# A planner's priorities for one block's chain, a seventh half piece beside it, and three unused matmuls fewer

## The chip, the cores and the metric

The kernel runs on one core of a Trainium2 chip. The metric is the device time of one execution in microseconds (us). Before the change it is 488.02 us, the median of three runs (486.81 to 488.70).

The engines that matter: TensorE (PE in the profile; PEld is its weight load), VectorE (DVE), ScalarE (ACT), GpSimd (POOL) and SyncE (SP), whose queue issues nearly all transfers.

## The reference

The operation has two halves. Half A is a convolution branch: `h = layernorm(x) * (1 + ca) + sa`, a short causal filter of four taps on `k`, `kv = k_shift * v`, a causal convolution of `kv` with a filter of length 2048 along the sequence (written with an FFT), and `x = x + ga * h * (conv + kv * ssm_D)`. Half B is a gated feed-forward network:

```
h   = layernorm(x) * (1 + cb) + sb
out = (silu(h @ w1) * (h @ w3)) @ w2
x   = x + gb * out
```

The six vectors sa, ca, ga, sb, cb, gb are the six parts of `silu(c) @ w_mod`. The sequence has 2048 rows of width 576, the hidden width is 4608, all in bf16.

## The kernel before

**Tiling.** The sequence is cut into eight blocks of 256 rows. The long convolution is done block by block in a small transform space: each block of `kv` gets a spectrum X (six rows of 576 per partition), each block of the filter a spectrum V, and block s of the result is the inverse transform of the sum over X[i] * V[s - i]. VectorE makes those products and sums (`pair`, tiles of 128x3456 elements: `p`, `z`), TensorE the forward and inverse transforms as matmuls with bases `Fk`, `Fb`, `Fi`.

The feed-forward half goes by row blocks of 512 rows, so two sequence blocks share one round r of four. In `stream`, w1 and w3 come in nine pieces of 512 columns (`wst` buffers 0, 1, 2, and in round 0 two more in the room of the spectra). For each piece TensorE makes gate and up in PSUM, ScalarE writes silu(gate) (`h`) and copies up (`u`), and VectorE multiplies them. In `down`, w2 comes in nine pieces of 288 KB per half of the output width, VectorE multiplies the result by gb (`og`, `gbrow`) and adds it to x. The matmuls of `stream` use half of the array's rows at a time: 64 rows, two of them side by side.

**The first round.** Round 0 needs block 0 and block 1. Only block 0 is ready early (`first_block`, an order written out by hand). So the stream of round 0 begins with half pieces: six of the nine w1/w3 pieces are run on the first 256 rows alone (matmuls of 256 columns), while block 1's convolution (`conv_second`) is in the works. When block 1's normalised rows (`h2row`) have been transposed by TensorE and written, scaled, to `h2T`, the same six pieces are run on rows 256 to 511, and the other three on all 512 rows. `FIRST` is the order in which round 0's `down` takes the hidden columns, `jobs` the order of the pieces.

**Block 1's chain.** `kv_rows` (VectorE) makes kv; `x_spectrum` (TensorE, copies by ScalarE) its spectrum; `x_sums`, `pair`, `real_parts` (VectorE) the product in transform space; `inverse` (TensorE); `residual_row` (VectorE, tiles `hg` and `x`); `quick_stats` (VectorE, GpSimd) and `normed` (VectorE) the rows `h2row`; `turn_split` and `turned_split` the transposes and the writing of `h2T`. Beside it, `filter_ahead(2)` makes the filter spectrum for block 2, and `mod_piece(5)` makes `gbrow` with ten matmuls of w_mod's last part, which `load_gb` brings into buffer 2.

**What sets the order.** After `first_block` all instructions are recorded and ordered by a planner (`_Recorder`). `relate` finds what each unit of work must come after. `weigh` gives the matmuls of the two streams (the lanes) their due times one after the other, and each other unit the latest start that its followers allow (`latest`). `search` runs `plan` a hundred times with noise on these due times and keeps the order with the best modelled time. `plan` fills each engine by readiness and then by `latest`. What comes out is a fixed order per engine; each engine works strictly in it and waits on semaphores. SyncE waits, for each transfer, on whatever last used the target and on the transfer eight places before it.

`mod_columns`, in `first_block`, turns two rows of the modulation into columns with small matmuls (`one,Wo` in the profile); `warm` puts matmuls before each of them whose result nobody reads (`shk`).

Of the kernel before, what the change touches and what calls it, by code (L numbers as in the profile page):

```python
# [22 lines left out]
H = 288  # L23
NF = F // P
RB = 512
NRB = S // RB
FC = 4
NW13 = 3
W2C = 4
N1 = 24  # L30
SPLIT = 2
AHEAD = 2
EPS = 1e-5
FIRST = (2, 3, 4, 5, 6, 0, 7, 1, 8)


def _ap(t, offset, dims):
# [173 lines left out]

class _Unit:
    def __init__(self, engine, n, fixed):
        self.engine, self.n, self.fixed = engine, n, fixed
        self.ops, self.pair = [], None
        self.lane, self.swap = False, None
        self.before, self.behind = set(), set()
        self.takes, self.uses = [], []
        self.start = self.end = None
        self.latest = float("inf")  # L220
        self.parts = []
# [16 lines left out]
class _Recorder:  # L238
# [23 lines left out]
    def __init__(self, tc):  # L262
        self.tc, self.nc = tc, tc.nc
        self.tiles, self.units = [], []
        self.fixed, self.open = True, None
        self.homes = {}
        for e in self.NAMES:
            setattr(self, e, _Engine(self, e))

    def add(self, op):  # L270
        u = self.open
        if u is None:
            u = _Unit(op.engine, len(self.units), self.fixed)
            self.units.append(u)
        assert u.engine == op.engine
        u.ops.append(op)

    @contextmanager
    def together(self, lane=False, swap=None):
        assert self.open is None  # L280
        self.open = u = _Unit("tensor", len(self.units), self.fixed)
        u.lane, u.swap = lane, swap
        self.units.append(u)
        try:
            yield u
        finally:
            self.open = None
# [63 lines left out]
    def relate(self):  # L351

        log = {}

        def meets(a, b):
            return a[1] < b[2] and b[1] < a[2] and any(x[0] < y[1] and y[0] < x[1] for x in a[3] for y in b[3])

        def inside(a, b):
            return b[1] <= a[1] and a[2] <= b[2] and all(any(y[0] <= x[0] and x[1] <= y[1] for y in b[3]) for x in a[3])
        for u in self.units:  # L360
            reads, writes = [], []
            for op in (u.pair[0] + u.pair[1] if u.pair else ()):
                op.measure()
            for op in u.ops:
                op.measure()
                reads += [r for r in map(self.spans, op.ins) if r]
                writes += [r for r in map(self.spans, op.outs) if r]
            seen = set()
            for kind, rs in ((0, reads), (1, writes)):
                for r in rs:  # L370
                    k = (kind, r[0], r[1], r[2], tuple(r[3]))
                    if k in seen:
                        continue
                    seen.add(k)
                    for v, s, wrote in log.get(r[0], ()):
                        if v is not u and (kind or wrote) and meets(r, s):
                            u.before.add(v)
            for r in writes:
                old = log.setdefault(r[0], [])
                old[:] = [x for x in old if x[0] is u or not inside(x[1], r)]  # L380
                old.append((u, r, True))
            done = set()
            for r in reads:
                k = (r[0], r[1], r[2], tuple(r[3]))
                if k not in done:
                    done.add(k)
                    log.setdefault(r[0], []).append((u, r, False))
            if u.swap is not None:
                u.before.add(u.swap)
        maker = {}  # L390
        for u in self.units:
            for x in u.takes:
                maker[x] = u
            if u.engine != "tensor":
                for x in u.uses:
                    m = maker[x]
                    if not m.fixed and not m.lane:
                        m.before |= {v for v in u.before if v.n < m.n}
        for u in self.units:
            for v in u.before:  # L400
                v.behind.add(u)
        lanes = [u for u in self.units if u.lane]
        for a, b in zip(lanes, lanes[1:]):
            b.previous = a
# [39 lines left out]
    def search(self):  # L444


        for u in self.units:
            u.wish = u.latest
        for x in self.tiles:
            x.uses = x.left  # L450
        best = None
        for n in range(self.TRIES):
            dice = random.Random(n)
            hold = dice.choice(self.HOLDS) if n else self.HOLD
            for u in self.units:
                u.latest = u.wish + (dice.gauss(0.0, self.NOISE) if n and not u.lane and u.engine != "sync" else 0.0)
            try:
                order = self.plan(hold)[1]
            except AssertionError:
                continue  # L460
            took = [self.plan(hold, order, *case)[0] for case in self.CASES]
            mean = sum(took) / len(took)
            if best is None or mean < best[0]:
                best = mean, order
        self.order = best[1]
        for _, _, u, _, _, at in self.order:
            for x, i in zip(u.takes, at):
                x.place = self.pairs[i]
        return best[0]
# [237 lines left out]
class _Kernel:  # L707
# [250 lines left out]
    def mod_columns(self):  # L958

        nc = self.nc  # L960
# [4 lines left out]
            yield  # L965
        ps = self.ps()
        for i in range(2):
            self.warm(3 - i, self.shk[:, 0, 0:512], ps)
            for j in range(6):
                lo = min(P * j, 512)  # L970
                n = P if j < 4 else 64
                at = 20 * i + 4 * min(j, 4)
                out = ps[0:n, 0, at:at + 4] if j < 5 else ps[64:P, 0, at:at + 4]
                nc.tensor.matmul(out, rows[:, i, lo:lo + n], self.one[0:1, 0:4], start=True, stop=True)
# [61 lines left out]
    def forward(self, basis, rhs, dst, more=()):  # L1036

        nc = self.nc
        for e in range(2):
            for cs in range(2):  # L1040
                ps = self.products([(basis[e][cc][:, cs], rhs[:, cc, :]) for cc in range(2)]
                                   + [(basis[e][0][0:1, cs], x) for x in more if cs == 0])
                out = dst(e, cs).rearrange("p (h d) -> p h d", h=2)
                nc.scalar.copy(out, ps[:, :, 0:H])
                yield 0.4

    def forward2(self, basis, rhs, both, odd, diff):

# [427 lines left out]
    def outcome(self, s, fill, waits, between=None, then=None, quick=False):  # L1476


        def steps():
# [15 lines left out]
            if quick:  # L1495
# [3 lines left out]
                    yield 1.25  # L1499
                for cc in range(2):  # L1500
                    self.normed(s, cc, *st[cc])
                    self.turned_split(self.turn_split(cc), 2 * s + cc)
                    yield 0.75
            else:
# [35 lines left out]

    def conv_second(self):
        yield from self.spectrum
        self.load_gb()
        self.pair_waves()
        self.keep_x(0)
        self.keep_v(0)
        self.load_taps(2)
        self.pair_taps(2)
        yield from self.gate_stats(1)
        yield from self.kv_rows(1)  # L1550
        yield from self.v_block(1)
        self.gate_var(1)
        yield from self.pair(self.X[0], self.V[1], 1)
        self.gate_shift(1)
        yield from self.x_spectrum(1)
        self.mod_piece(5)
        self.gate_rows(1)
        yield from self.gate(1)
        yield from self.x_sums(1)
        self.load_taps(3)  # L1560
        yield from self.pair(self.X[1], self.V[0], 1)
        yield from self.outcome(1, self.mix(self.filter_ahead(2)), (5.0, 3.5, 0.0, 2.0), quick=True)
        self.load_kv(2)
        yield 0.0

    def conv(self, s0):
# [10 lines left out]
        def old():  # L1577
            if s0 < NBLK - 2:
                V, X = self.old_v(s0 - 1, s0), self.old_x(1, s0)
                yield from self.pair(X, V, s0)  # L1580
                for j in range(2, s0):
                    X = self.old_x(j, s0)
                    yield from self.pair(X, V, s1)
# [198 lines left out]
    def run(self):  # L1782
# [2 lines left out]
        self.early_loads()  # L1785
        self.first_block()
        rec.fixed = False
        n1 = N1 // FC
        self.stream(0, [(fc, 0, 256, b) for fc, b in enumerate((0, 1, 3, 4, 0, 1))])
        self.run_all(self.conv_second())  # L1790
        jobs = [(fc, 256, 512, None) for fc in (2, 3, 4, 5)]
        new = [(n1 + i, 0, RB, b) for i, b in enumerate((2, 1, 2))]
        again = [(fc, 256, 512, b) for fc, b in enumerate((0, 0))]
        while new or again:
            jobs += new[0:1] + again[0:1]
            new, again = new[1:], again[1:]
        for r in range(NRB):
            if r > 0:
                bufs = [b if b == 2 else (r + b) % 2 for b in (0, 1, 2, 0, 1, 2, 0, 1, 0)]
# [66 lines left out]
```

## Time and profile before

| What | Value |
|---|---|
| median of three runs | 488.02 us |
| the profiled execution's own time | 488.18 us |
| its span, first to last instruction | 486.3 us |
| TensorE busy | 478.1 us, 98% |
| VectorE busy | 336.7 us, 69% |
| ScalarE busy | 288.4 us, 59% |
| granted TensorE clock | 1.000 |
| DMA, mean over the span | 217 GB/s |

The share of busy time is not even. From 80 to 160 us VectorE is busy for 9 to 10 tenths of each slice; in the last quarter, where only weights are streamed, for one or two tenths. The DMA engines are full from 10 to 35 us and again around 120 to 155 us.

How to read the lines that follow: a line of a timeline has the start, the duration, the engine, the operation with the tile it writes and those it reads, the shape and the count, and in brackets the idle time before it with what ended it. A line of waits has the total, the number and the longest. A line of issues has the size of one and the median time from issue to landing. All instructions recorded by the planner carry the line of its helper, L207, so tiles tell them apart.

### The profile page before, as it was taken

How to read it: one execution, taken by the hardware profiler on the slowest of the kernel's cores; microseconds unless marked ns; L12 is line 12 of the kernel's file. 1: busy time of each engine (PE TensorE's matmuls, PEld its weight loads, DVE VectorE, ACT ScalarE, POOL GpSimd, SP SyncE). 2: the span in 40 equal slices, each digit the busy share in tenths (PEclk: the TensorE clock that was granted, in tenths of full speed). 3: DMA queues.
4: the chain of work that ended last, by engine and by line, in shares of the span. 5: the costliest groups of instructions: out<-in, count | busy, mean ns of one | idle time of the engine just before them, and what ended most of it. 6: DMA issues, size and time to landing. Idle time of an engine off the chain costs nothing.

```text
span 486.3 us, 11220 instructions
## 1 busy us (share of the span) xinstructions
PE 478.1 (98%) x4696; PEld 321.5 (66%) x4697; DVE 336.7 (69%) x457; ACT 288.4 (59%) x565; POOL 25.8 (5%) x45
## 2 busy tenths in 40 slices
PE   9999999999999999999999899999999999999996
PEld 3668788666776444445776688777777444445775
DVE  7887989999999789979698895999732211211012
ACT  6788488964872779787430667987670455555000
POOL 4220000000200000010200000000000000000000
PEclk9999999999999999999999999999999999999999
DMA  8999676667899974689999999462767435371640
GB/s 211 341 344 268 211 239 186 195 197 193 223 269 316 351 268 140 213 263 367 301 244 262 290 285 345 129 195 99 209 165 174 132 120 185 114 228 50 194 123 24
DMA packets 115195, 105.32 MB, mean 217 GB/s; under 512 B 22533, under 2 KB 108871, under 8 KB 115146
## 3 DMA queue, kind: packets, MB, share of 16 engines
q1 hardware_dynamic: 114998, 104.33, 70.6%
q8 instruction: 36, 0.59, 0.5%
q10 hardware_dynamic: 148, 0.30, 0.2%
q14 instruction: 13, 0.11, 0.1%
HBM read 89.07 MB, written 9.44 MB: 203 GB/s over the span
## 4 chain that ended last, share of the span: by engine, by line
PE 90%; DVE 5%; ACT 2%; DMA 1%; issue 0%; SPq 0%; POOL 0%; DVEq 0%
PE ps L207 90%; DMA kT<-knat 1%; DVE z L207 1%; DVE p L207 1%; DVE hg L207 1%; DVE og L207 1%; DVE x L207 1%; ACT hg L207 0%; ACT h L207 0%; ACT h2T L207 0%; DVE bnst L207 0%; SPq L207 0%; ACT u L207 0%; DVE h L207 0%; ACT spectra L207 0%
## 5 line engine op out<-in xcount | busy, mean ns | idle before, releaser
L207 PE MATMUL ps<-h2T,wst 64*128 64x512 bf16 (+1 forms) x2736 | 278.3, 354 | 0.1
L207 PEld LDWEIGHTS <-wst 64*128 64x128 bf16 x2736 | 156.2, 94 | 102.7 <-issue 2.0
L207 PE MATMUL ps<-wst,h 128*128 128x288 bf16 x1152 | 143.9, 286 | 0.3 <-DVE og L207 0.2
L207 PEld LDWEIGHTS <-h 128*128 128x128 bf16 x1152 | 112.4, 98 | 30.6 <-issue 2.4
L207 ACT CAST u<-ps 128x512 bf16<-128x512 f32 x144 | 84.0, 584 | 68.8 <-PE ps L207 68.3
L207 ACT ACTIVATE h<-ps 128x512 bf16<-128x512 f32 x144 | 86.5, 600 | 52.5 <-PE ps L207 52.5
L207 DVE TENSOR_TENSOR h<-h,u 128x1024 bf16<-128x1024 bf16 x72 | 49.6, 690 | 74.0 <-ACT h L207 53.7
L207 DVE TENSOR_TENSOR p<-spectra 128x3456 bf16<-128x3456 bf16 x28 | 54.7, 1952 | 0.2
L207 DVE TENSOR_TENSOR z<-z,p 128x3456 bf16<-128x3456 bf16 x28 | 54.7, 1952 | 0.2
L207 ACT ACTIVATE junk<-x 128x576 bf16<-128x576 bf16 x56 | 38.5, 688 | 14.2 <-DVE x L207 13.7
L207 DVE TENSOR_TENSOR og<-ps,gbrow 128x576 bf16<-128x576 f32 (+1 forms) x18 | 12.4, 689 | 38.0 <-PE ps L207 37.4
L207 POOL TENSOR_TENSOR lnr<-lnv,neghalf 128x2 f32<-128x2 f32 x13 | 13.9, 1073 | 296.5 <-DVE lnv L207 277.6
L207 DVE TENSOR_TENSOR spectra<-spectra 128x1152 bf16<-128x1152 bf16 (+1 forms) x35 | 25.6, 735 | 0.7 <-ACT spectra L207 0.4
L207 ACT CAST spectra<-ps 128x576 bf16<-128x576 f32 x34 | 21.7, 647 | 4.0 <-PE ps L207 4.0
L207 PE MATMUL ps<-kT,Fk 64*128 64x288 bf16 (+1 forms) x116 | 20.7, 306 | 2.0 <-DMA kT<-knat 1.4
L207 PEld LDWEIGHTS <-Fb 64*128 64x128 bf16 (+1 forms) x248 | 16.7, 95 | 7.2 <-DVE var L207 0.2
L207 PE MATMUL ps<-kv,Fb 64*128 64x288 bf16 (+1 forms) x144 | 20.6, 283 | 0.0
L207 DVE TENSOR_TENSOR z<-z 128x1152 bf16<-128x1152 bf16 x26 | 19.3, 750 | 0.0
L207 PE MATMUL ps<-h2T,spectra 64*128 64x256 bf16 x288 | 17.6, 269 | 0.2 <-ACT h2T L207 0.2
L207 ACT ACTIVATE h2row<-x,lnn,lnr 128x576 bf16<-128x576 bf16 (+1 forms) x24 | 13.9, 642 | 5.7 <-DMA h2T<-h2row 3.9
L207 DVE TENSOR_TENSOR z<-spectra 128x3456 bf16<-128x3456 bf16 (+1 forms) x9 | 15.8, 1761 | 0.1
L207 PEld LDWEIGHTS <-spectra 64*128 64x128 bf16 x288 | 14.9, 94 | 1.5 <-DVE h2T L207 0.2
(106 smaller groups left out, 275.6 us busy)
## 6 DMA issues: line engine op xcount, KB each, us to landing
wst<-in_B_w_dram SPq DMA_DIRECT2D x72, 512.0 KB, 4.4
wst<-in_B_w_dram SPq DMA_DIRECT2D x72, 288.0 KB, 4.0
kh<-in_A_k_dram SPq DMA_DIRECT2D x7, 720.0 KB, 6.8
wst<-in_B_w_dram SPq DMA_DIRECT2D x72, 64.0 KB, 4.0
spectra<-Xd SPq DMA_DIRECT2D x5, 864.0 KB, 7.3
spectra<-Vd SPq DMA_DIRECT2D x5, 864.0 KB, 7.7
Xd<-spectra SPq DMA_DIRECT2D x4, 864.0 KB, 5.7
Vd<-spectra SPq DMA_DIRECT2D x4, 864.0 KB, 7.5
```

The lines of the kernel that those rows point to most:

```text
L207: getattr(getattr(nc, self.engine), self.method)(*[_real(a) for a in self.args], **{k: _real(v) for k, v in self.kw.items()})
```

## The change

- `_Unit` gets two fields. `haste` is taken from a unit's due time in `search` (`u.wish = u.latest - u.haste`); it is 4000 ns (`HASTE`) for what `conv_second` records from block 1's `gate_stats` to the end of its `outcome`, and 0 otherwise. `fence` names one unit that a VectorE unit must come after; `relate` adds it to what the unit waits for.
- The unit that makes block 1's second `h2row` is kept as `self.turned`, and the first products of block 2 (in `conv(2)`) get it as fence.
- `filter_ahead(2)` and the load of taps 3 are recorded after block 1's `outcome` and no longer mixed into it.
- The stream beside block 1 has seven half pieces; the seventh goes into buffer 2. `jobs` and `FIRST` follow: the second halves of pieces 2, 3, 6, 5, 4, then piece 7 whole, the second half of 0, piece 8 whole, the second half of 1.
- `load_gb` and `mod_piece(5)` are recorded before the stream, not inside `conv_second`.
- `mod_columns` has one unused matmul before each group, where it had three and two.
- `forward`, in the call with the ssm_D row (`more`), takes its four products in another order, those with that row last.

```diff
-N1 = 24
-FIRST = (2, 3, 4, 5, 6, 0, 7, 1, 8)
+HASTE = 4000.0
+FIRST = (2, 3, 6, 5, 4, 7, 0, 8, 1)
...
+            u.haste = self.haste
+            u.fence = self.fence if op.engine == "vector" else None
...
+            if u.fence is not None:
+                u.before.add(u.fence)
...
-            u.wish = u.latest
+            u.wish = u.latest - u.haste
...
-            self.warm(3 - i, self.shk[:, 0, 0:512], ps)
+            self.warm(1, self.shk[:, 0, 0:512], ps)
...
-        for e in range(2):
-            for cs in range(2):
+        for e, cs in ((0, 1), (1, 1), (0, 0), (1, 0)) if more else ((0, 0), (0, 1), (1, 0), (1, 1)):
...
                     self.normed(s, cc, *st[cc])
+                    self.turned = self.rec.units[-1]
...
     def conv_second(self):
         yield from self.spectrum
-        self.load_gb()
...
         self.pair_taps(2)
+        self.rec.haste = HASTE
         yield from self.gate_stats(1)
...
-        self.mod_piece(5)
...
         yield from self.x_sums(1)
+        yield from self.pair(self.X[1], self.V[0], 1)
+        yield from self.outcome(1, (), (5.0, 3.5, 0.0, 2.0), quick=True)
+        self.rec.haste = 0.0
         self.load_taps(3)
-        yield from self.pair(self.X[1], self.V[0], 1)
-        yield from self.outcome(1, self.mix(self.filter_ahead(2)), (5.0, 3.5, 0.0, 2.0), quick=True)
+        yield from self.filter_ahead(2)
...
+                self.rec.fence = self.turned if s0 == 2 else None
                 yield from self.pair(X, V, s0)
+                self.rec.fence = None
...
-        n1 = N1 // FC
-        self.stream(0, [(fc, 0, 256, b) for fc, b in enumerate((0, 1, 3, 4, 0, 1))])
+        self.load_gb()
+        self.mod_piece(5)
+        self.stream(0, [(fc, 0, 256, b) for fc, b in enumerate((0, 1, 3, 4, 0, 1, 2))])
         self.run_all(self.conv_second())
-        jobs = [(fc, 256, 512, None) for fc in (2, 3, 4, 5)]
-        new = [(n1 + i, 0, RB, b) for i, b in enumerate((2, 1, 2))]
-        again = [(fc, 256, 512, b) for fc, b in enumerate((0, 0))]
-        while new or again:
-            jobs += new[0:1] + again[0:1]
-            new, again = new[1:], again[1:]
+        jobs = [(fc, 256, 512, None) for fc in (2, 3, 6, 5, 4)]
+        jobs += [(7, 0, RB, 2), (0, 256, 512, 1), (8, 0, RB, 0), (1, 256, 512, 2)]
```

More of the change, by code (lines that the diff above doesn't have):

```diff
@@ L213, in __init__ @@
     def __init__(self, engine, n, fixed):
-        self.engine, self.n, self.fixed = engine, n, fixed
+        self.engine, self.n, self.fixed, self.haste, self.fence = engine, n, fixed, 0.0, None
         self.ops, self.pair = [], None
@@ L264, in __init__ @@
         self.tiles, self.units = [], []
-        self.fixed, self.open = True, None
+        self.fixed, self.open, self.haste, self.fence = True, None, 0.0, None
         self.homes = {}
@@ L281, in together @@
         self.open = u = _Unit("tensor", len(self.units), self.fixed)
-        u.lane, u.swap = lane, swap
+        u.lane, u.swap, u.haste = lane, swap, self.haste
         self.units.append(u)
@@ L1038, in forward @@
         nc = self.nc
-        for e in range(2):
-            for cs in range(2):
[L1041 to L1045, printed above, removed]
+        for e, cs in ((0, 1), (1, 1), (0, 0), (1, 0)) if more else ((0, 0), (0, 1), (1, 0), (1, 1)):
+            ps = self.products([(basis[e][cc][:, cs], rhs[:, cc, :]) for cc in range(2)]
+                               + [(basis[e][0][0:1, cs], x) for x in more if cs == 0])
+            out = dst(e, cs).rearrange("p (h d) -> p h d", h=2)
+            nc.scalar.copy(out, ps[:, :, 0:H])
+            yield 0.4
     def forward2(self, basis, rhs, both, odd, diff):
```

## The prediction

> **What bounds the kernel now.** I read five views in this order: the page's busy times, the waits of TensorE, its timeline around the edit, VectorE's timeline there, and the sizes and landing times of transfers.
>
> ```profile
> PE 478.1 (98%) x4696; PEld 321.5 (66%) x4697; DVE 336.7 (69%) x457; ACT 288.4 (59%) x565; POOL 25.8 (5%) x45
> ...
> PE ps L207 <- DMA kT<-knat: 1.4, 1, 1.4
> PE ps L207 <- DVE h2T L207: 1.2, 1, 1.2
> PE ps L207 <- ACT h2T L207: 0.7, 2, 0.5
> PE ps L207 <- DVE h2row L207: 0.6, 2, 0.4
> PE ps L207 <- DVE og L207: 0.2, 1, 0.2
> ```
>
> TensorE is the bound: 98% busy, and all its listed waits together are 4.1 us. Nothing that leaves its work alone can gain much. A busy share hides slow stretches, so I also compared each stretch of its timeline with a dense pitch from dense rows: 0.0546 us per 64-row matmul of 256 columns (100 in 5.46), 0.108 of 512 columns, 0.0613 of 288, 0.1225 per full-array matmul of 288. Between the start of the w1/w3 stream (31.22) and the end only three places fall behind: 58.7 to 63.6 us, 129 to 137 us, and 270 us.
>
> ```profile
> 25.64 0.82 PE L207 MATMUL ps<-shk 128*128 128x512 bf16 x2
> 26.39 0.37 PE L207 MATMUL ps<-one,Wo 1*128 1x4 bf16 x6
> 26.69 0.61 PE L207 MATMUL ps<-shk 128*128 128x512 bf16 x2
> 27.23 0.37 PE L207 MATMUL ps<-one,Wo 1*128 1x4 bf16 x6
> 27.53 0.66 PE L207 MATMUL ps<-kT,Fk 128*128 128x288 bf16 x4
> ...
> 58.74 1.95 PE L207 MATMUL ps<-h2T,wst 64*128 64x256 bf16 x26
> 61.12 0.68 PE L207 MATMUL ps<-moved,h2row 128*128 128x128 bf16 x6 [0.43 <-DVE h2row L207]
> 61.99 0.68 PE L207 MATMUL ps<-moved,h2row 128*128 128x128 bf16 x6 [0.19 <-DVE h2row L207]
> 62.70 0.65 PE L207 MATMUL ps<-kT,Fk 128*128 128x288 bf16 x4
> 63.57 0.61 PE L207 MATMUL ps<-h2T,spectra 64*128 64x256 bf16 x8 [0.22 <-ACT h2T L207]
> ```
>
> The `shk` rows are the unused matmuls. At 61 us the stream has run out of first-half pieces and waits for block 1's transposed rows. On VectorE just before:
>
> ```profile
> 53.79 1.95 DVE L207 TENSOR_TENSOR z<-spectra 128x3456 bf16<-128x3456 bf16 x1
> 55.66 0.68 DVE L207 TENSOR_TENSOR h<-h,u 128x1024 bf16<-128x1024 bf16 x1
> 56.26 0.75 DVE L207 TENSOR_TENSOR hg<-ps,hg 128x576 bf16<-128x576 f32 x1
> ```
>
> The 1.95 us product is block 2's, standing in front of block 1's `hg`. Last, the transfers that answer for the third place and for a rival below:
>
> ```profile
> 271.56 0.28 PE L207 MATMUL ps<-kT,Fk 64*128 64x288 bf16 x1 [1.37 <-DMA kT<-knat]
> ...
> wst<-in_B_w_dram SPq DMA_DIRECT2D x72, 288.0 KB, 4.0
> ```
>
> **The change, part by part.** The sum is made against the profiled execution: 488.18 us, a span of 486.3 and 1.88 around it; the median of the runs shown is 488.02, 0.16 less. The new order of each engine is read from the built program.
>
> *Fewer unused matmuls.* Three of five go. In front of the first six `one,Wo` stand three (25.64 to 26.39: 0.25 each), in front of the second two (0.27 each). The first row that they cover is copied by ScalarE by 25.75, the second by 26.37. With one each, the first six start at 25.91, end at 26.21, one matmul to 26.48, the second six end at 26.8 instead of 27.53. Behind them the transposes' rows are ready at 26.73 and 27.29, ScalarE's copies idle 1.27 before, and VectorE idles 1.32 for TensorE, so all follows: **-0.73**. Bounds: 0 if a transfer holds the stream (w1/w3 piece 0 was issued by 17.5 and lands 8.1 later, before 30.5: no), -0.8 for all three.
>
> One rule speaks against this. The Trainium skill, "TensorE: Matmul & The Clock Gate", Why this matters for your kernels: idle gaps of over about 3 us put the array back to half its clock. The row: the longest TensorE gap in this stage is 0.45, and the granted clock stands at its top in every slice, so the rule would not fire; if it did, by the page's 3.4 us window at half rate, the sum would be an estimated 1.7 us worse.
>
> *Order of the first spectrum.* The same 20 matmuls and four copies, the ssm_D row later: 0, since all four copies are read together at 15.09, 2.9 us after the last.
>
> *gb early.* Its three loads (648 KB) move in SyncE's queue past piece 3, and past pieces 4 and 5. At the 390 GB/s of 20 to 30 us that is 1.7 us; the transfers fall quiet at 35.0, now 36.7. Piece 3 is used at 44.5, piece 4 only waits for buffer 0 anyway (35.8 before): hidden, with 8 us of cover. Without that cover each microsecond is one of TensorE. The ten matmuls (57.42 to 58.6) move from the end of the chain to about 41.5, ScalarE's copy with them: same price, moved.
>
> *Block 1's chain.* Stream start is now 30.49. Up to the last kv product the order holds 188 stream matmuls (10.26), 32 kv (1.96) and gb (1.2 and two switches, 0.2): 44.1, before 46.2. VectorE's kv needs no product of the stream's `h` in between and is ready at 37.4, TensorE arrives at 37.6. ScalarE then sets the pace: two `hg` from 41.85 (1.54), the wave 0.65, gb's copy 0.55, one pair `h`,`u` 0.98, the last spectrum copy 0.64: 46.2, where VectorE began at 47.07 before. From there sums 0.78, product 1.97, `h` 0.6, addition 1.97, real parts 1.45: 52.97. TensorE reaches the inverse at 52.6, so it waits 0.35. The inverse takes 1.6 (16 matmuls of 0.0613, 8 of the stream between, 0.17 to come out): `hg` at 54.55 instead of 56.26. The fence is what empties that place; the urgency puts the rest first. To the two `h2row` it took 4.4 and 5.7 us; with the new order of the small steps and an `h` between them 4.7 and 6.35: rows at 59.2 and 60.9. TensorE is at the first transposes after 424 stream matmuls at 59.3, at the second, 16 stream matmuls later, at 60.9. Then 64 stream matmuls are left, 3.5 us, while the last `h2T` is written after block 2's 1.87 us product, at 64.4; TensorE comes at 65.4. Waits in all 0.45.
>
> Before, 58.74 to 63.57 held 28 stream matmuls (1.53), 12 transposes (0.105 each) and four of 0.1225: 3.28 of 4.83, so 1.55 lost, 0.25 of it switches that remain: 1.3 of waiting. **-0.85**. Bounds: -1.3 with no wait; +1.0 if work of 1.87 us stands in front of the rows again, as the product did before.
>
> *Seventh piece.* 144 matmuls of 256 instead of 72 of 512: 7.86 against 7.78, **+0.08**; the 72 additional weight loads (94 ns) lie beside.
>
> *Switches* between half and full array: 36 instead of 32, 0.10 each (56.83 to 57.42 holds 0.49 of matmuls and 0.10 more): **+0.4**.
>
> *What comes free next.* The spectrum of block 2 ahead leaves the chain and runs in its wake; kv of block 2 is ready at about 71, used at 75. VectorE has, by its durations, 65.9 us of work between block 1's rows and block 3's `x` in both orders, and starts it 1.0 us sooner. The end of the first half of `down` comes at about 132.7, `og` is then next on VectorE. Before, `og` came 1 us late (134.40 behind a 1.95 product) and 129 to 140 lost 0.88. I take **-0.5**: bounds -0.88 and +1.0, if VectorE lags instead, nearer the first by the 1.0 just counted.
>
> *kT at 270 us.* SyncE issues it behind a weight load that waits for TensorE; 58 matmuls of 512 lay between that release and the use, now 64: 0.65 more cover for a stall of 1.6. **-0.65**, bounds -1.6 and +0.7 (a landing of 6.5 instead of the 5.8 of that window).
>
> Sum: -0.73 - 0.85 + 0.08 + 0.4 - 0.5 - 0.65 = -2.25: **485.9 us**.
>
> **Rivals.** *The chain is no earlier.* ScalarE, 88% busy from 31 to 47, delays the last spectrum copy by the 0.9 us I count as won, and the later gains go with it; the unused matmuls remain: -0.73 + 0.48, 487.9. For it: I have ScalarE itself as the limit. Against it: the product before `hg` is gone whatever ScalarE does.
>
> *The first w2 piece comes late* (slower). Buffer 0 is now freed by piece 8, with only a half piece behind it: 72 matmuls, 4.0 us to the first `down` matmul, where a whole piece gave 8.8. Against it: that piece landed 2.9 after its issue and the median is 4.0, so it is just in time. For it: weight pieces landed 8.1 and 9.2 after issue at 12 to 30 us, when the queues were full. At 9.2 TensorE waits 5.2: 491.1. Below 4.0 it costs nothing, at 6.3 the gain is gone.
>
> *More is won.* The kT stall goes wholly and nothing waits at 61: 485.9 - 0.95 - 0.45 = 484.5.
>
> **How the numbers follow.** A measurement of this kernel can tell about 0.5% (2.44 us) from no change: 485.58 and 490.46 are the limits. Forecast 0.60, its own range 484.8 to 487.2 from the bounds of the terms, 0.24 of it under the limit; no earlier 0.20, all the same; late w2 0.12, slower; more won 0.08, faster. So faster 0.32, same 0.56, slower 0.12. The range runs from 484.3 to 490.0: it holds forecast, chain and most of the last case, and leaves out the rest of that and the late piece.
>
> **What would show it.** The `one,Wo` rows should end at 26.8; `hg` of block 1 start near 54.6; the waits for h2row be under 0.3 in all; the kT wait under 1.0; no wait for wst near 111. A wait for wst there, or `og` waits above 1 us, makes the prediction wrong, and so does a pause at 44 to 46, where a PSUM pair for the stream is freed by gb's copy only 0.1 us before use.

## The result and the profile after

The changed kernel takes 486.10 us, the median of 22 runs (483.86 to 489.33); the kernel before, timed beside it on the same chip, 486.81 (485.04 to 491.62). The ratio is 0.9988, with a 95% interval of 0.9970 to 1.0006: no difference that can be measured. The prediction was 485.9 us, with no measurable difference as the likeliest outcome. But it had been made against an execution of 488.18 us, as a change of -2.25 us; against the kernel before beside it, the change measured is -0.7 by the medians, and in a second comparison (below) +1.2. So the number was met in part by luck: the kernel before, run more often, is itself 1.4 to 2.8 us below the execution that the sum started from. Why that is, and which terms of the sum were real, is what the runs below are for.

The profiled execution after takes 485.60 us with a span of 483.8, 2.5 us less than the one of before. Its busy line and the waits of TensorE:

```profile
PE 476.5 (99%) x4770; PEld 303.0 (63%) x4770; DVE 336.4 (70%) x457; ACT 288.1 (60%) x565; POOL 28.1 (6%) x45
...
PE ps L207 <- DMA wst<-in_B_w_dram: 1.5, 1, 1.5
PE ps L207 <- DVE h2T L207: 1.2, 1, 1.2
PE ps L207 <- ACT h2T L207: 0.5, 1, 0.5
```

The waits for `h2row`, `og` and `kT` are gone. A wait of 1.5 us for a piece of w2 is new. The other two come before 28 us, in both kernels. Three stages of TensorE's timeline answer for the steps of the prediction. First the rows with the unused matmuls (`shk`):

```profile
21.51 2.92 PE L207 MATMUL ps<-h,u 128*128 128x288 bf16 x20
24.36 0.39 PE L207 MATMUL ps<-shk 128*128 128x512 bf16 x1
24.68 0.37 PE L207 MATMUL ps<-one,Wo 1*128 1x4 bf16 x6
24.98 0.39 PE L207 MATMUL ps<-shk 128*128 128x512 bf16 x1
25.31 0.37 PE L207 MATMUL ps<-one,Wo 1*128 1x4 bf16 x6
25.61 0.66 PE L207 MATMUL ps<-kT,Fk 128*128 128x288 bf16 x4
```

From the last `h,u` row to the `kT,Fk` behind the second `one,Wo` it takes 4.10 us (21.51 to 25.61), before 4.75 (22.78 to 27.53). But the whole group lies 1.3 to 1.9 us earlier, and 1.27 of that is already there at the `h,u` row, in front of anything that this step touches. Next, block 1's chain on VectorE and where TensorE takes up its rows:

```profile
53.39 0.76 DVE L207 TENSOR_TENSOR hg<-ps,hg 128x576 bf16<-128x576 f32 x1 [0.85 <-PE ps L207]
...
57.42 0.41 DVE L207 TENSOR_SCALAR h2row<-x,bnmv,bnr 128x576 bf16<-128x576 bf16 x1
...
59.18 0.43 DVE L207 TENSOR_SCALAR h2row<-x,bnmv,bnr 128x576 bf16<-128x576 bf16 x1 [0.44 <-POOL bnr L207]
```

```profile
55.04 3.22 PE L207 MATMUL ps<-h2T,wst 64*128 64x256 bf16 x56
58.19 0.85 PE L207 MATMUL ps<-moved,h2row 128*128 128x128 bf16 x6
...
61.41 3.25 PE L207 MATMUL ps<-h2T,wst 64*128 64x256 bf16 x52
64.49 1.25 PE L207 MATMUL ps<-h2T,spectra 64*128 64x256 bf16 x20
```

The transposes come with no bracket: TensorE still had stream matmuls when the rows were ready, and went on with 52 more until the second halves began at 64.49. Last, the new wait, in TensorE's row and in SyncE's queue (start, duration of the issue):

```profile
137.83 8.74 PE L207 MATMUL ps<-wst,h 128*128 128x288 bf16 x70
148.04 4.08 PE L207 MATMUL ps<-wst,h 128*128 128x288 bf16 x32 [1.47 <-DMA wst<-in_B_w_dram]
```

```profile
137.33 2.45 SPq L207 DMA_DIRECT2D wst<-in_B_w_dram  x4
140.83 1.22 SPq L207 DMA_TRANSPOSE h2T<-h2row  x1
142.14 0.53 SPq L207 DMA_DIRECT2D wst<-in_B_w_dram  x1
142.77 1.51 SPq L207 DMA_TRANSPOSE h2T<-h2row  x1
```

The single load at 142.14 is the piece of w2 that TensorE waits for. It lands 5.90 us after its issue. Four places in buffer 2 hold these pieces in turn, so 48 matmuls, 5.9 us at the dense pitch, lie between the release of a place and its next use. This place was free at about 140.7 (146.57 less 5.88); SyncE, which stood at the transpose, issued the load 1.45 us later, and that is the wait.

**The two kernels by stages.** The start of the `h,u` row of 10 (ten matmuls early in `first_block`) is taken as zero, since nothing ahead of it but the order of the first spectrum was changed. The marks are the first stream matmul, the first w2 matmul of round 0, the first stream matmul of round 1, the first w2 matmul of rounds 1 and 2, and the end of the span. A column is the time between two marks in us; the last two go by the span, which is read to 0.1.

| Kernel, one execution each | `h,u` at | to stream 0 | to w2 of round 0 | to stream 1 | to w2 of round 1 | to w2 of round 2 | to the end | `h,u` to end |
|---|---|---|---|---|---|---|---|---|
| before | 13.58 | 17.64 | 82.89 | 39.20 | 74.45 | 111.97 | 146.57 | 472.7 |
| before, again | 11.43 | 17.64 | 82.90 | 39.20 | 75.72 | 110.63 | 146.58 | 472.7 |
| before, other first spectrum | 12.70 | 17.65 | 82.89 | 39.20 | 74.44 | 110.51 | 146.61 | 471.3 |
| after | 12.30 | 17.00 | 81.62 | 41.13 | 75.10 | 110.56 | 146.09 | 471.5 |
| after, again | 10.92 | 17.09 | 81.62 | 41.06 | 75.24 | 110.55 | 146.02 | 471.6 |
| after, six pieces | 12.65 | 16.99 | 83.20 | 38.64 | 75.45 | 111.05 | 146.12 | 471.5 |
| after, no urgency | 12.58 | 16.99 | 82.25 | 39.06 | 76.14 | 109.95 | 146.53 | 470.9 |
| the same, again | 12.11 | 16.99 | 82.26 | 39.11 | 76.11 | 109.95 | 146.57 | 471.0 |
| the same, kT first | 11.40 | 16.99 | 82.26 | 39.94 | 74.94 | 109.95 | 146.52 | 470.6 |

Two things are read from it. The stages up to w2 of round 0 repeat within 0.1 us, so these columns carry conclusions from one execution; the start and the stages behind carry them less, as the runs below show. And of the change itself: it wins 0.64 us to stream 0 and 1.27 up to w2 of round 0, and has lost 1.93 by stream 1. There the two kernels stand level, counted from the `h,u` row.

Some work also changed stages. Counted at the pitches of the prediction (an estimate, with 0.105 us per transpose and 0.10 per switch), the matmuls of the three stages from stream 0 on take 81.1, 38.3 and 74.5 us before, and 80.6, 39.3 and 75.0 after. What is lost beside them is 1.8, 0.9 and 0.0 before, and 1.0, 1.8 and 0.1 after. So of the 1.93 us lost by stream 1, 1.0 is work that moved there.

### The profile page after: what moved, and what is told of

It is laid out like the page before. It is cut to its first block, busy times and chain, and to the rows that moved or that the text cites. A ratio compares the mean times of both kernels' runs of the same rounds, so it can differ in the third digit from the quotient of the medians.

```text
span 483.8 us, 11365 instructions
## 1 busy us (share of the span) xinstructions
PE 476.5 (99%) x4770; PEld 303.0 (63%) x4770; DVE 336.4 (70%) x457; ACT 288.1 (60%) x565; POOL 28.1 (6%) x45
## 4 chain that ended last, share of the span: by engine, by line
PE 97%; DMA 1%; DVE 1%; ACT 1%; issue 0%; DVEq 0%
PE ps L207 97%; DMA wst<-in_B_w_dram 1%; DVE og L207 0%; ACT h2T L207 0%; DVE x L207 0%; ACT h L207 0%; ACT W L207 0%; ACT u L207 0%; DVE h2T L207 0%; DVEq L207 0%
## 5 line engine op out<-in xcount | busy, mean ns | idle before, releaser
L207 PEld LDWEIGHTS <-wst 64*128 64x128 bf16 x2808 | 141.0, 94 | 117.6 <-PE ps L207 1.2
L207 DVE TENSOR_TENSOR h<-h,u 128x1024 bf16<-128x1024 bf16 x72 | 49.6, 689 | 69.2 <-ACT h L207 39.3
L207 POOL TENSOR_TENSOR lnr<-lnv,neghalf 128x2 f32<-128x2 f32 x13 | 16.0, 1236 | 295.1 <-DVE lnv L207 295.1
L207 PE MATMUL ps<-kT,Fk 64*128 64x288 bf16 (+1 forms) x120 | 18.9, 300 | 0.5 <-ACT h2T L207 0.5
L207 PE MATMUL ps<-kv,Fb 64*128 64x288 bf16 (+1 forms) x136 | 18.6, 284 | 0.1
L207 DVE TENSOR_TENSOR kv<-kv,p 128x1152 bf16<-128x1152 bf16 x21 | 15.8, 753 | 0.1
```

The costliest lines, as they stand in the source:

```text
L207: getattr(getattr(nc, self.engine), self.method)(*[_real(a) for a in self.args], **{k: _real(v) for k, v in self.kw.items()})
```

## The experiments

**The changed kernel again, and the first spectrum alone.** The open question was the 1.28 us at the `h,u` row. Theory A: it belongs to the execution; theory B: to the edit of `forward`. The first run alters nothing.

> The changed kernel once more, nothing altered. In its first profile TensorE went from half pace (0.25 us per full-array matmul of 288 columns) to full pace (0.123) at about 9.0 us, in the kernel before's only at about 11.0 us, and its h,u row of 10 matmuls began at 12.30 instead of 13.58: 1.28 us of the 2.5 between the two profiles. Theory A (it is the execution): the pace changes at another moment here, anywhere from 7 to 12 us, h,u begins more than 0.3 us away from 12.30, and the profile's time moves by that much. Theory B (the edit did it): h,u begins at 12.30 within 0.1 again. On both: no wait for h2row or h2T at 57 to 64 us, no wait at 270 us, one wait for wst near 147 us of 1.0 to 2.0 us, and a ratio to the kernel before of 0.997 to 1.0006 as in the first comparison.

The second is the kernel before with this edit only:

```diff
-        for e in range(2):
-            for cs in range(2):
+        for e, cs in ((0, 1), (1, 1), (0, 0), (1, 0)) if more else ((0, 0), (0, 1), (1, 0), (1, 1)):
```

> The kernel before with the order of the first spectrum alone (the two parts without the ssm_D row first). Theory A (the moment of full pace belongs to the execution): ratio 1.000 within 0.002, and h,u begins where its pace happened to change, not systematically at 12.3. Theory B (the order brings full pace earlier): h,u at 12.3 within 0.1 and 1.28 us less, ratio 0.9974. The prediction had put this edit at 0.

Measured: the changed kernel again 486.62 us median of 12 against 485.42 of the kernel before, ratio 1.001 (0.9988 to 1.0032); the first spectrum alone 485.87, ratio 0.9997 (0.9977 to 1.0018). The `h,u` rows begin at 10.92 and 12.70. TensorE's rows at the start, of the kernel before:

```profile
6.06 1.17 PE L207 MATMUL ps<-kT,Fk 128*128 128x288 bf16 x4
7.16 0.66 PE L207 MATMUL ps<-knat,Fk 1*128 1x288 bf16 x2
7.75 2.10 PE L207 MATMUL ps<-kT,Fk 128*128 128x288 bf16 x8
...
13.58 1.49 PE L207 MATMUL ps<-h,u 128*128 128x288 bf16 x10
```

and of the changed kernel's second execution:

```profile
5.68 1.63 PE L207 MATMUL ps<-kT,Fk 128*128 128x288 bf16 x12 [0.15 <-DMA kT<-in_A_ssm_k_dram]
...
10.92 1.49 PE L207 MATMUL ps<-h,u 128*128 128x288 bf16 x10
```

Eight `kT,Fk` matmuls in 2.10 us are 0.26 each, twelve in 1.63 are 0.13: half pace and full pace of the same instruction, and the granted clock reads 1.00 in both. Theory A holds: over 14 executions `h,u` began anywhere from 10.92 to 13.58, the changed kernel's alone at 12.30 and 10.92, the kernel before's at 13.58 and 11.43. So the 1.28 us need no edit to explain them, and the edit alone shows no gain.

**The kernel before once more**, for its profile.

> The kernel before once more, for its profile alone. Theory A (start and kT stall belong to the execution): the h,u row of 10 begins anywhere from 10.9 to 13.6, and the wait of 1.37 for kT at 270 us is there or not; with it 472.7 from the h,u row to the end, without it 471.3. If both belong to the program: 13.58 and 1.37 again within 0.1.

`h,u` at 11.43. The wait for `kT` at 270 us is not there; one of nearly the same kind is somewhere else, in TensorE's timeline:

```profile
159.20 0.44 PE L207 MATMUL ps<-kT,Fk 64*128 64x288 bf16 x2 [0.94 <-DMA kT<-knat]
```

In the run with the first spectrum alone, whose program is the kernel before's from 13 us on, no wait for `kT` is listed at all. So three executions of the same instructions had 1.37 at 270 us, 0.94 at 159 us, and none. From `h,u` to the end it is 472.7 with either, and 471.3 without. The expectation had only the first and the last case; a wait that moves was not in it.

**Fewer unused matmuls alone**, in the kernel before.

```diff
-            self.warm(3 - i, self.shk[:, 0, 0:512], ps)
+            self.warm(1, self.shk[:, 0, 0:512], ps)
```

> The kernel before with one unused matmul in front of each set of six one,Wo matmuls instead of three and two. The prediction's step: from the end of the h,u row of 20 to the first kT,Fk behind the one,Wo rows it takes 1.16 us instead of 1.89 (-0.73); 1.25 in the changed kernel's profile. If the gain lasts to the end: 0.65 to 0.73 us less, ratio 0.9985 to 0.9987. Rival: it is given back where the stream waits for block 1's rows at about 61 us, whose waits (0.43, 0.19, 0.22 before) grow by as much, ratio 1.000.

Measured: 486.34, ratio 1.0019 (0.9993 to 1.0045). The stage to stream 0 takes 17.10 instead of 17.64, so 0.54 is won there. The planner, with other starting times, chose another order behind it: TensorE waits 1.11 for `h2row` at 59 us, and 0.51 and 0.22 for `og` at 133 to 134. The stages to w2 of round 0 and to stream 1 take 83.36 and 40.20, so 0.47 and 1.00 are given back. The rival was right: what TensorE wins early is more than spent behind it. The listed waits for block 1's rows and for `og` grow by 0.8 in all; the rest of the 1.47 stands in no listed wait.

**No urgency, no fence, but seven pieces.** Theory C, the prediction's, says that urgency and fence take the waits at 61 us away; theory D says that the seventh piece covers them, that is, puts stream matmuls between the moment when the rows are asked for and the moment when TensorE needs them.

```diff
-HASTE = 4000.0
+HASTE = 0.0
...
-                self.rec.fence = self.turned if s0 == 2 else None
+                self.rec.fence = None
```

> The changed kernel without the urgency of block 1's chain and without the fence, but with seven pieces beside it. Theory C (the prediction's: urgency and fence take the waits away): block 2's first product of 1.95 us stands in front of block 1's hg again, the rows come 1.5 to 3 us later, and TensorE waits for h2row or h2T by 1.0 us or more in all between 58 and 66 us; the time is 1.0 us or more above the changed kernel's of this call. Theory D (the seventh piece's 72 more first-half matmuls, 3.9 us, are the cover that counts): the waits between 58 and 66 us stay below 0.3 us in all, and the time is the changed kernel's within 0.5 us.

Measured: 484.86, ratio to the kernel before 0.9972 (0.9949 to 0.9995). VectorE's timeline of this kernel, and the only wait of TensorE there:

```profile
51.03 1.95 DVE L207 TENSOR_TENSOR z<-spectra 128x3456 bf16<-128x3456 bf16 x1
52.90 0.68 DVE L207 TENSOR_TENSOR h<-h,u 128x1024 bf16<-128x1024 bf16 x1
53.50 0.75 DVE L207 TENSOR_TENSOR hg<-ps,hg 128x576 bf16<-128x576 f32 x1
...
57.52 0.41 DVE L207 TENSOR_SCALAR h2row<-x,bnmv,bnr 128x576 bf16<-128x576 bf16 x1
```

```profile
60.52 0.67 PE L207 MATMUL ps<-moved,h2row 128*128 128x128 bf16 x6 [0.20 <-DVE h2T L207]
```

Block 2's product of 1.95 us stands in front of `hg` again, as it did before the change, and costs nothing: `hg` and the first `h2row` begin 40.92 and 44.94 us after `h,u`, with urgency and fence 41.09 and 45.12. VectorE ends block 1's `z` 1.1 us sooner here, counted from `h,u`, and the 0.85 us for which it idles in front of `hg` in the changed kernel (above) are filled; the two make room for the product. TensorE waits 0.20. Theory C falls, and D stands on the waits. On the time it does not: D said the changed kernel's within 0.5 us, and the median is 1.8 us below that of the changed kernel in the same comparison (486.62). From `h,u` to the end one execution each shows 0.6 of it; the late piece of w2 is no longer there (0.15 at 146.7), and a wait of 0.87 for `kT` is.

**Six pieces, with urgency and fence.**

```diff
-FIRST = (2, 3, 6, 5, 4, 7, 0, 8, 1)
+FIRST = (2, 3, 4, 5, 6, 0, 7, 1, 8)
...
-        self.stream(0, [(fc, 0, 256, b) for fc, b in enumerate((0, 1, 3, 4, 0, 1, 2))])
+        self.stream(0, [(fc, 0, 256, b) for fc, b in enumerate((0, 1, 3, 4, 0, 1))])
...
-        jobs = [(fc, 256, 512, None) for fc in (2, 3, 6, 5, 4)]
-        jobs += [(7, 0, RB, 2), (0, 256, 512, 1), (8, 0, RB, 0), (1, 256, 512, 2)]
+        jobs = [(fc, 256, 512, None) for fc in (2, 3, 4, 5)]
+        jobs += [(6, 0, RB, 2), (0, 256, 512, 0), (7, 0, RB, 1), (1, 256, 512, 0), (8, 0, RB, 2)]
```

> The changed kernel with six pieces of w1/w3 beside block 1's chain and the kernel before's order of pieces behind it, with the urgency and the fence kept. Theory C (urgency and fence suffice): the waits for h2row and h2T between 56 and 66 us are below 0.5 us in all, and the time is the changed kernel's. Theory D (the 72 matmuls of 3.9 us that the seventh piece puts there are the cover): 1.0 to 2.5 us of waits there, and from the h,u row to the end more than without the urgency (470.9).

Measured: 486.00, ratio 0.9993 (0.9973 to 1.0013). In TensorE's timeline the wait is back in front of the second halves, although the transposes begin 1.7 us sooner than in the changed kernel (44.17 after `h,u` instead of 45.89):

```profile
61.89 3.23 PE L207 MATMUL ps<-h2T,spectra 64*128 64x256 bf16 x56 [1.09 <-DVE h2T L207]
```

What TensorE waits for is in VectorE's timeline:

```profile
57.42 0.43 DVE L207 TENSOR_SCALAR h2row<-x,bnmv,bnr 128x576 bf16<-128x576 bf16 x1 [0.66 <-POOL bnr L207]
...
59.13 1.95 DVE L207 TENSOR_TENSOR z<-spectra 128x3456 bf16<-128x3456 bf16 x1
61.00 0.84 DVE L207 TENSOR_SCALAR h2T<-ps,cbcol,sbcol 128x128 bf16<-128x128 bf16 x3
```

The fence holds block 2's product behind the second `h2row`, and there it now stands in front of the last `h2T`. In the changed kernel it stands at the same place (60.28) and the seventh piece hides it. So the fence has not taken the product out of the way, it has moved it from one step of block 1's chain to a later one. Six pieces without the fence, the rest of the change kept, were not run. The stage to w2 of round 0 takes 83.20 instead of 81.62; 0.65 of that is work that moved there, and beside the work counted as above 1.9 is lost instead of 1.0. That is theory D's 1.0 or more. But the time is the changed kernel's all the same (471.5 from `h,u` to the end): the stage to stream 1 has 0.7 less work and no late piece of w2 (38.64 instead of 41.13), and the stage behind it loses 0.8 more.

**What makes the piece of w2 late: three moves, and one of the loads.** In the changed kernel's second execution the wait was there again, 1.40 us, so it belongs to the program. Theory E: a 1.95 us product on VectorE holds GpSimd's `lnr`, block 3's `h2row` comes late, SyncE's transpose of it waits, and the load of w2 behind it too. Theory F: the transfer itself is slow. Each kernel is the changed one with single units of work moved in the finished order, nothing else:

```diff
         self.order = best[1]
+        for what, behind in moves:
+            at = {u.n: k for k, (_, _, u, _, _, _) in enumerate(self.order)}
+            if at[what] < at[behind]:
+                self.order.insert(at[behind], self.order.pop(at[what]))
```

The numbers are units of work in the order of their recording. The first kernel moves the product `p` behind `lnn` (`moves` is `((1127, 803),)`), the second block 3's first transpose behind the w2 load (`((809, 627),)`), the third does both.

> The changed kernel with one VectorE instruction moved: the product p of 1.95 us at 136.88 goes behind lnn of block 3, so that nothing runs on VectorE while GpSimd computes lnr. Chain that is supposed: the product holds GpSimd's lnr (2.27 us beside it, 0.7 to 1.2 without), so h2row of block 3 comes 1.1 to 1.5 us late, SyncE's transpose of it holds the w2 load behind it, and TensorE waits 1.40 to 1.47 us for that piece at 147. Theory E (this chain): lnr takes 0.7 to 1.2 us, h2row begins 1.1 to 1.5 us sooner, the w2 wait falls below 0.5, and the time from the start of the h,u row of 10 to the span's end falls from 471.5 to 470.2 to 470.7. Theory F (the transfer itself is slow, 5.86 us from issue to landing): the wait stays above 1.0.

> The changed kernel with one SyncE instruction moved: the first transpose of block 3's h2row goes behind the load of the w2 piece that came late; GpSimd's lnr and h2row stay as late as they are. Theory E (SyncE's queue holds the load): it is issued 1.0 to 1.5 us sooner and the wait for wst falls below 0.5, but block 3's last h2T, which ended at 151.16 where TensorE needed it at 152.05, now ends later and TensorE comes sooner: a new wait for h2T of 0.3 to 1.0 near 151; from the h,u row to the end 470.7 to 471.3. Theory F (slow transfer): the wait stays above 1.0.

> Both moves together. Theory E: no wait for wst above 0.3 near 147 and none for h2T near 151; from the h,u row of 10 to the span's end 470.0 to 470.4 instead of 471.5, ratio to the kernel before 0.996 to 0.999. Theory F: 471.3 to 471.7.

Measured: ratios 1.0016 (0.9990 to 1.0042), 0.9988 (0.9960 to 1.0017) and 0.9988 (0.9968 to 1.0009). GpSimd's `lnr` with the product beside it (the changed kernel) and without (the first move):

```profile
137.10 2.27 POOL L207 TENSOR_TENSOR lnr<-lnv,neghalf 128x2 f32<-128x2 f32 x1 [5.40 <-DVE lnv L207]
```

```profile
137.69 0.69 POOL L207 TENSOR_TENSOR lnr<-lnv,neghalf 128x2 f32<-128x2 f32 x1 [5.40 <-DVE lnv L207]
```

The first links of theory E are right: 0.69 instead of 2.27, and `h2row` begins 0.9 and 1.3 us sooner in the two kernels with this move. The last link is not. In the first kernel SyncE is still issuing the four w1/w3 loads when the row is ready; the w2 load goes out 0.25 us sooner and lands 7.15 us after, and TensorE waits longer (in an execution that is itself 2.6 us above this kernel's median of 486.81):

```profile
149.63 5.75 PE L207 MATMUL ps<-wst,h 128*128 128x288 bf16 x32 [2.47 <-DMA wst<-in_B_w_dram]
```

With the transpose moved, this piece is in time, and the next one, behind the transposes now, is late by 1.18 us (148.65), and by 1.19 with both moves. From `h,u` to the end the three take 474.7, 471.8 and 472.7, so none gains on 471.5, and theory E's 470.0 to 471.3 came in no run. Neither VectorE nor the place of one load decides alone. What goes with it is seen in the transfer engines of the changed kernel between 136 and 151 us, in 40 slices of 0.375 us (busy share in tenths, then GB/s):

```profile
DMA  4999952967999678789992399999400799997977
GB/s 89 290 281 275 275 103 25 71 156 246 360 391 333 210 123 186 238 287 302 295 142 80 53 237 204 342 280 169 15 11 14 173 303 300 390 590 295 571 313 306
```

They are busy most of the time, and then almost idle from 146.5 to 147.6, at 11 to 15 GB/s, 3.7 us after block 3's second transpose was issued; the w2 piece lands at 148.0. The same hole, two to five slices at 25 GB/s or less between 144 and 149 us, is there in nine executions of the seven kernels with the seventh piece, which issue the transposes among or behind those loads. The kernel with six pieces (two slices, 7 and 28 GB/s, with no wait for w2) and the one with fewer unused matmuls alone (five, 14 to 37) do so too, and have it less deep. In the three executions of the kernel before and of the one with the other first spectrum, which issue both transposes ahead of the w2 loads, no two slices in a row are under 50 GB/s. That a transposing transfer makes the others pause fits all of them, but no run isolates it.

The last run of this row takes the four w1/w3 loads out of the way (theory G: they stand ahead of the w2 piece; theory H: they do not matter), with `moves` `((839, 630), (840, 630), (838, 630), (837, 630))`:

> The changed kernel with the four loads of w1/w3 for round 1 (1.15 MB) moved on SyncE behind the two w2 pieces and block 3's transposes; nothing else moves. Moving h2row or the transpose alone left the wait for wst at 2.47 and 1.18 us, with the transfer engines busy all the time from 125 to 155 us. Theory G (the w2 piece lands late because those four loads stand ahead of it in the transfer queues): it lands 4 to 5 us after its issue instead of 5.9, the wait for wst falls below 0.4, and from the start of the h,u row of 10 to the span's end it takes 469.9 to 470.4 instead of 471.5. Theory H (the four loads matter nothing, the transposes of h2row and the small packets fill the queues): the wait stays above 1.0.

Measured: 486.44, ratio 1.0009 (0.9990 to 1.0029). TensorE's waits behind 140 us:

```profile
145.93 4.08 PE L207 MATMUL ps<-wst,h 128*128 128x288 bf16 x32 [0.56 <-DMA wst<-in_B_w_dram]
...
159.19 0.51 PE L207 MATMUL ps<-kT,Fk 64*128 64x288 bf16 x2 [0.88 <-DMA kT<-knat]
...
217.30 6.43 PE L207 MATMUL ps<-h2T,wst 64*128 64x512 bf16 x57 [0.59 <-DMA wst<-in_B_w_dram]
```

The piece lands 5.0 us after its issue and the wait falls to 0.56, so most of it goes with those loads, as G says. But 0.88 for `kT` and 0.59 for a later piece come in its place, and from `h,u` to the end it is 472.6, 1.1 more than the changed kernel. In each of these four orders some load was late. That the transfer engines as such are the limit is not shown: in this last run SyncE stood at block 3's transpose and issued no load, and from 136.8 to 140.9 us the engines moved 0 to 15 GB/s.

**The kernel without urgency again, and with kT first.** To see whether it beats both kernels, it ran a second time, and once with the four `kT` loads ahead of three loads of w1/w3 on SyncE that wait for TensorE (`moves` `((866, 1116), (864, 1116), (863, 1116))`).

> The changed kernel without urgency and fence once more (0.9972 of the kernel before, 0.9949 to 0.9995, the first time). If that was a property of the program: ratio below 1 again, 0.995 to 0.999, from the h,u row to the end 470.9 within 0.3, and again a wait of 0.5 to 1.0 for kT near 158 us. If it was the executions: a ratio of 0.999 to 1.002.

> The changed kernel without urgency and fence, and on SyncE the four loads of kT ahead of the three loads of w1/w3 that wait for TensorE. Expected: the wait for kT near 158 us (0.87) is gone, from the h,u row to the end 470.0 to 470.3, ratio to the kernel before 0.9955 to 0.998. Rival: another wait takes its place in the same stretch, 470.7 to 471.2.

Measured: 484.72, ratio 0.9981 (0.9964 to 0.9998), and 484.56, ratio 0.9971 (0.9957 to 0.9985). The wait for `kT` (0.87 and 0.83 in the two executions without the move) is gone, the stage to w2 of round 1 takes 74.94 instead of 76.14 and 76.11. In this execution a wait for `h2T` was longer than in the others, where it was 0.47 and none, with the same order up to there:

```profile
150.59 6.44 PE L207 MATMUL ps<-h2T,wst 64*128 64x512 bf16 x58 [1.31 <-ACT h2T L207]
```

From `h,u` to the end it is 470.6, between the expected 470.0 to 470.3 and the rival's 470.7 to 471.2. It has the lowest median of this study, 0.29% below the kernel before, 0.15 to 0.43; the interval overlaps that of the kernel without the move.

## Why the prediction was right or wrong

No measurable difference is what came, and the time was within 0.2 us, but only some of the terms were right.

- **Fewer unused matmuls, -0.73.** Measured -0.54 to -0.65 at stream 0. The term was a little too large. It took 0.25 and 0.27 us per unused matmul, the mean of each group. But from start to start an inner one takes 0.22 to 0.23 and the last one, in front of `one,Wo`, 0.31, and the last ones stay: three inner ones are 0.67. In three of the eleven executions with this edit the first `one,Wo` begins 0.1 later, 0.05 to 0.06 behind the end of ScalarE's first copy. (Seven of their traces list a wait of 0.26 in front of the second `one,Wo`; there the row of the unused matmul is missing from the trace, and that `one,Wo` begins no later than in the others.) "VectorE idles for TensorE, so all follows" did not hold to the end: alone, the edit was given back by stream 1.
- **Order of the first spectrum, gb early, seventh piece: 0, 0, +0.08.** Nothing contradicts them: alone, the first spectrum gives 0.9997, the pause feared at 44 to 46 us is not there, and the counted work grows by 0.5 from the start of the stream to the end, as the 0.08 and the switches' 0.4 say. They were terms of TensorE's work. What the seventh piece is worth as cover was not among them.
- **Block 1's chain, -0.85.** The loss up to w2 of round 0 fell from 1.8 to 1.0, so the size was right. Counted from the start of the stream, `hg` came at 24.09 against the predicted 24.06, the rows were ready at 28.5 and 30.3 against 28.7 and 30.4. The cause was wrong. The step that failed is "the fence is what empties that place; the urgency puts the rest first": without both the rows are as early, and with both but only six pieces 1.09 us is waited, for an `h2T` behind the very product that the fence moved. What covers it is the seventh piece's 72 matmuls, 3.9 us. Why the chain itself came earlier without them (the early gb, the recording order without the filter spectrum in between) was not separated.
- **What comes free next, -0.5, bounds -0.88 and +1.0.** The `og` waits went, as said: counted from `h,u`, `og` began at 119.03 instead of 120.82, and 129 to 137 us is dense. But the stage lost 0.9 more than before, at the edge of the bound. The step that failed asked only whether VectorE keeps up. The next late thing was a piece of w2: TensorE came to the end of round 0 sooner, and block 3's first transpose was issued 3.1 us later than before, counted from `h,u` (128.5 instead of 125.4), with the load behind it.
- **kT at 270 us, -0.65.** It took one execution's stall for the program's. The cover of 64 matmuls against 58 is beside the point: the same program had the stall at 270, at 159, or not at all.
- **The rival of the late w2 piece, 0.12.** Wrong at its place: the first piece, with 4.0 us of cover, came in time at 110.92. Its mechanism came true some 36 us later, where a place had 5.9 us of cover and the load used 1.45 of them standing behind a transpose.
- **The base.** 488.18 us held a late full pace at the start (`h,u` at 13.58, where other executions of that kernel have 11.43 and 12.70) and the `kT` stall. In four comparisons the kernel before has medians of 486.81, 485.42, 485.69 and 485.67. Against those the change was worth -0.7 in one comparison and +1.2 in the other (ratios 0.9988 and 1.001, both intervals with 1 in them): as good as nothing. Two errors, a base too high and a gain too large, cancelled and made the number right.

The prediction weighed the idle-gap rule of the Trainium skill, "TensorE: Matmul & The Clock Gate". It did not fire: the twelve `kT,Fk` matmuls behind those rows take 1.63 us before and after. That the granted clock stood at its top says nothing here, since it reads 1.00 at half pace too (below). The longest wait of TensorE in any run is 2.5 us, so no run tests the rule's 3 us.

## What to carry to other kernels

A stall or a slow start in one profiled execution is not yet a property of the kernel: look for it in a second execution before it is put into a sum. When a stage is made shorter on the bound engine, ask for each transfer behind it what its cover will then be, as here, where, moved work left out, 1.4 us were won up to 111 us and 0.9 of them lost again by 152 us, most of it to a load that came no sooner. And when several edits go together, the cheap one (72 more matmuls in the right place) may do what the elaborate one is credited with.

## What the runs showed of the hardware

**The start at half pace.** TensorE takes 0.24 us from the start of one `kT,Fk` matmul to the next at first, and 0.12 to 0.13 later. In six of 14 executions full pace was there by 5.7 us, in the others it came between about 8.5 and 11.8, though TensorE had hardly idled since its first matmul at 1.17. The granted clock in the profile shows 1.00 throughout. The Trainium skill, "TensorE: Matmul & The Clock Gate", Part 1: The HAM clock gate, tells of a free-running window of 3.4 us and a transition point that varies by 0.5 us either way. These runs agree that it varies with the execution, but over some 6 us, from before 5.7 to about 11.8, and it is worth up to 2.7 us at the `h,u` row, more than anything that this change did.

**GpSimd beside VectorE.** Over the 14 executions a `lnr` of 2 values per partition takes 0.69 to 0.83 us, 1.05 to 1.20 where a VectorE operation of about 0.75 us on two SBUF tiles began shortly before it, and 2.27 to 2.94 where one of 1.95 us did; one of 3.61 had three such operations in a row beside it. The Trainium skill, "SBUF — State Buffer", SBUF: two separate sides, calls the port pair that the two engines share an exclusive lock, held for a whole instruction, which a GpSimd operation that reads SBUF and a VectorE operation with two SBUF inputs both need. The run with the product moved away agrees: 2.27 became 0.69.

**Transposing transfers.** Where block 3's `h2T<-h2row` was issued among or behind the loads, in nine executions of the kernels with seven pieces, the transfer engines had a hole of 0.75 to 1.9 us at 25 GB/s or less within 1 to 5 us, in a stretch that mostly runs at 100 to 400. Shown as something that comes with them, not why.
